# One PSUM tile takes its bank from another pool, and the sigmoid table is loaded in a later block

## The chip, the cores and the metric

The kernel runs on one core of one Trainium2 chip. The metric is the device time of one execution in microseconds (us). The engines are named as in the profile: PE (TensorE matmuls), PEld (its weight loads), DVE (VectorE), ACT (ScalarE), POOL (GpSimd) and SP (SyncE, which issues the DMAs here). Each engine works through its own instructions in order; it waits for the others by semaphores.

## What is computed

An attention (2 batches, 8 heads, 768 positions, 64 per head; each query sees a window of keys and 24 block summaries) is followed by two MLPs over 1536 tokens, all in float32:

```python
def _moe_ref(x, w_in, w_out):            # first MLP
    h = np.maximum(x @ w_in, 0.0)        # 1536x512 @ 512x2048
    return (h * h @ w_out)               # 1536x2048 @ 2048x512

def _moe2_ref(x, w_in, w_out):           # second MLP
    h = x @ w_in
    g = h * (1.0 / (1.0 + np.exp(-h)))
    return (g @ w_out)

def reference(...):
    attn_out = _attn_ref(q, k, v)        # scores, exp, normalise, times v
    x = attn_out.transpose(0, 2, 1, 3).reshape(B * S, H * D)
    return _moe2_ref(_moe_ref(x, ...), ...)
```

## The kernel before

Every float32 factor is split into a high and a low part, and each product is three matmuls (high by high, high by low, low by high).

The first MLP is done in three token blocks of 512 columns. `first_block` (block 1 of 3, to about 151 us) runs the attention for its own tokens and the 16 chunks of the MLP beside it; its order is written out by a planner (`first_order`). `layer1_block(1, ...)` (the second block, to about 257 us) runs beside the rest of the attention, and `layer1_block(2, ...)` (the third block, to about 350 us) runs beside the decoding of the second MLP's weights (`prefetch`). In each chunk m a product `h` (12 matmuls, PSUM pool `ps_h`) goes through ACT and DVE into `g`, and two chunks later `g` times `wo` is added into four accumulators (`ps_acc`). The last accumulations of the third block are kept back in the list `fill`.

The second MLP runs over 16 steps q: eight pairs of 128 hidden columns for each of two token groups of 768. Its first product uses seven half-size products of a Strassen-like scheme, which run in a chain through two or three PSUM tiles per step: `hx` (products 11, s2, s3 and 22), `hz` (s1 and s4) and `hy` (12). Each product is six matmuls of 128x384; `evacuate` copies the intermediate states of the chain to SBUF (ACT, tiles `e`), DVE adds them, and `silu` makes four quarters of `g` (sigmoid on ACT, a multiplication on DVE, high part on ACT, low part on DVE). The last quarter, `s21`, reads `hx` itself, so `hx` is in use until the DVE multiplication of `s21`. Between the products, `between` puts the accumulations of the step before, `rows(q-1, k)` for k = 0 to 5, or in step 0 the pieces kept in `fill`. `rows` multiplies the quarters of `g` by `wq`, the split of the second MLP's output weights (`load2`: a DMA, high part on ACT, low part on DVE). `ready` splits the weights of the next step into `r` (high part on ACT, low part on DVE).

PE's order in the third block and the second MLP is the order in which the code is written; the order of ACT and DVE there is a scheduler's.

PSUM has eight banks, in three pools (lines 238 to 240), and a tile here fills one:

```python
ps_h   = ... bufs=2     # h of the first MLP; hx, hz, hy of the second
ps_acc = ... bufs=4     # accumulators, k = 0, 1, 2, 5 in the second MLP
ps_att = ... bufs=2     # attention; accumulators k = 3, 4 in the second MLP
```

A new tile of a pool waits until the last reader of the bank's former tile is done.

ACT evaluates its functions from a loaded table. Line 902, `act.activation(out=share[:, 0:1], in_=share[:, 0:1], func=AF.Sigmoid)`, is written ahead of the third block and computes nothing that is used: `share` is a small constant tile whose readers are done by then. It is there so that a table with the sigmoid is loaded. It depends on little, and the order of the built kernel has it early in the first block.

Of the kernel before, what the change touches and what calls it, by code (L numbers as in the profile page):

```python
# [10 lines left out]
F32 = mybir.dt.float32  # L11
F32R = mybir.dt.float32r
AF = mybir.ActivationFunctionType
# [9 lines left out]
P = 128  # L23
# [27 lines left out]
HALF = 384  # L51
# [157 lines left out]
def kernel(  # L209
# [17 lines left out]
    vec, act, pool, pe, sp = nc.vector, nc.scalar, nc.gpsimd, nc.tensor, nc.sync  # L227
# [10 lines left out]
    ps_h = ctx.enter_context(tc.tile_pool(name="ps_h", bufs=2, space=PSUM))  # L238
    ps_acc = ctx.enter_context(tc.tile_pool(name="ps_acc", bufs=4, space=PSUM))
    ps_att = ctx.enter_context(tc.tile_pool(name="ps_att", bufs=2, space=PSUM))  # L240
# [9 lines left out]
    def tt(eng, o, a, b, op):  # L250
        return eng.tensor_tensor(out=o, in0=a, in1=b, op=op)  # L251

    def sub(eng, o, a, b):
        return tt(eng, o, a, b, ALU.subtract)
# [26 lines left out]
    def raw_wi(w, m, name):  # L281
        load_raw(w[m].rearrange("p k f -> p (k f)"), f"{name}{m}")
# [4 lines left out]
    def dec_scale(name):  # L287
        c = ws_p.tile([P, DM], I32, tag="c", name=f"c_{name}")

        copy(act, c.bitcast(F32), raws[name][:, :, 1].bitcast(F32), scale=2.0 ** -112)  # L290
        return c

    def dec_low(name):
        low = raws[name][:, :, 0]
        vec.tensor_scalar(out=low, in0=low, scalar1=29, scalar2=None, op0=ALU.logical_shift_right)

    def dec_sign(name):
        low, high = raws[name][:, :, 0], raws[name][:, :, 1]
        vec.scalar_tensor_tensor(out=low, in0=high, scalar=SIGN, in1=low,  # L299
                                 op0=ALU.bitwise_and, op1=ALU.bitwise_or)  # L300
# [45 lines left out]
    share = share_p.tile([P, PHASE - 8], F32, tag="share", name="share")  # L346
# [147 lines left out]
    def att_steps():  # L494
        for i in range(NFIRST - 1, NG + 2):
            if NFIRST <= i - 2 < NG:
                products(i - 2)
                x_high(i - 2)
                x_low(i - 2)
            if i + 1 < NG:  # L500
                kw_load(i + 1)
                q_load(i + 1)
                side_by_side(i + 1)
                k_sums(i + 1)
            if NFIRST <= i < NG:
                v_load(i)
            yield
            if NFIRST <= i - 1 < NG:
                transposes(i - 1)
                a_copy(i - 1)  # L510
            yield
            if NFIRST <= i < NG:
                scores(i)
                minima(i)
                exps(i)
                guard(i)
                inverse(i)
                norm(i, vec)
            yield

    att = att_steps()
# [62 lines left out]
    def first_block():  # L584
# [172 lines left out]
        finish1(0, accs)  # L757

    def layer1_block(bi, steps, prefetch, last=None):
        n = BLOCKS[bi]  # L760
        x = xt[bi]
# [33 lines left out]
    def keep_decoded(j):  # L795
        name = f"wp{j}"
        raw_wo(w_out2, j, "wp")
        c = dec_scale(name)
        dec_low(name)
        dec_sign(name)  # L800
        dec_join(name, c)
        sp.dma_start(out=scr2[j], in_=c.bitcast(F32))
# [68 lines left out]
    def decode_pair(m):  # L871
        p, half = m // 2, m % 2
        name = f"wj{m}"
        if not half:
            us[p] = wi_p.tile([P, 2, 2, 2 * P], F32, tag="wi", name=f"u{p}")
        raw_wi(w_in2, m, "wj")
        c = dec_scale(name)
        dec_low(name)
        dec_sign(name)
        u = us[p]  # L880
        vec.scalar_tensor_tensor(out=u[:, half].rearrange("p a c -> p (a c)").bitcast(I32), in0=c, scalar=3, in1=raws.pop(name)[:, :, 0],
                                 op0=ALU.logical_shift_left, op1=ALU.bitwise_or)
        if half:
            v = vs[p] = wi_p.tile([P, 3, 2 * P], F32, tag="wi", name=f"v{p}")
            tt(pool, v[:, 0], u[:, 1, 0], u[:, 1, 1], ALU.add)
            sub(pool, v[:, 1], v[:, 0], u[:, 0, 0])
            sub(pool, v[:, 2], u[:, 0, 1], v[:, 1])
            sub(pool, u[:, 1, 0], u[:, 0, 0], u[:, 1, 0])

    parts = build(lambda name: raw_p.tile([P, 2, HALF], F32, tag="raw", name=name))  # L890

    def prefetch(m):
        decode_pair(m)
        if m >= 3 and m - 3 < 5:
            parts[m - 3]()
        elif m == 8:
            parts[5]()
        if m >= 10 and FIRST2 + DEC1 <= FIRST2 + DEC1 + m - 10 and DEC1 + m - 10 < NF:
            keep_decoded(DEC1 + m - 10)

    fill = [None]
    act.activation(out=share[:, 0:1], in_=share[:, 0:1], func=AF.Sigmoid)
    with tc.manual_schedule(engines={pe.engine}):
        layer1_block(2, 0, prefetch, fill)
        fill = fill[1:]
        xt2_ctx.close()
# [21 lines left out]
        def product(o, q, x, first):  # L928
            r, f = ring.pop((q, x)), forms[TIMES[x]].bitcast(F32R)
            for kk in range(2):  # L930
                w = slice(kk * P, kk * P + P)
                mm(o, r[:, 0, w], f[:, 0, kk], start=first and kk == 0, stop=False, skip_group_check=not first)
                mm(o, r[:, 0, w], f[:, 1, kk], start=False, stop=False, skip_group_check=not first)
                mm(o, r[:, 1, w], f[:, 0, kk], start=False, stop=kk == 1, skip_group_check=not first)
            ready(q + 1, x)

        def evacuate(src, name):
            e = ev_p.tile([P, HALF], F32, tag="ev", name=name)
            copy(act, e, src)
            return e  # L940

        def silu(src, g, cols, name):
            s = s_p.tile([P, HALF], F32, tag="s", name=name)
            act.activation(out=s, in_=src, func=AF.Sigmoid)  # L944
            tt(vec, s, src, s, ALU.mult)
            on_act = copy(act, g[:, 0, cols], s)
            marks_done.append((on_act, sub(vec, g[:, 1, cols], s, g[:, 0, cols].bitcast(F32))))
# [3 lines left out]
        def load2(n):  # L951
            if n < 2 * NF:
                c = c_p.tile([P, DM], F32, tag="c", name=f"c2_{n}")
                sp.dma_start(out=c, in_=scr2[n % NF])
                w = wo2[n] = w_p.tile([P, 2, DM], F32R, tag="w", name=f"wq{n}")
                with behind(1):
                    split(w, c, vec)
# [18 lines left out]
        def between(q, ks):  # L976
            if q > 0:
                for k in ks:
                    rows(q - 1, k)
            elif fill:  # L980
                fill.pop(0)()
# [14 lines left out]
        def again(x):  # L996
            sp.dma_start(out=forms[x], in_=kept[list(TIMES.values()).index(x)])
# [8 lines left out]
        for q in range(2 * NPAIR):  # L1006
            for i in range(2):
                gs[q, i] = gq_p.tile([P, 2, 2 * HALF], F32R, tag="g", name=f"g{q}_{i}")

            def after(i):  # L1010
                if q == NPAIR - 1:
                    again(TIMES[CHAIN[i]])

            xx = ps_h.tile([P, HALF], F32, tag="h", name=f"hx{q}")
            product(xx, q, "11", True)
            r1 = evacuate(xx, f"e1_{q}")
            after(0)
            z = ps_h.tile([P, HALF], F32, tag="h", name=f"hz{q}")
            product(z, q, "s1", True)
            r5 = evacuate(z, f"e5_{q}")  # L1020
            after(1)
            between(q, [3])
            product(xx, q, "s2", False)
            r2 = evacuate(xx, f"e2_{q}")
            after(2)
            product(z, q, "s4", False)
            tt(vec, r2, z, r2, ALU.add)
            silu(r2, gs[q, 0], b, f"s12_{q}")
            after(3)
            load2(2 * q)  # L1030
            between(q, [4, 5])
            product(xx, q, "s3", False)
            tt(vec, r5, xx, r5, ALU.add)
            silu(r5, gs[q, 1], b, f"s22_{q}")
            after(4)
            z = ps_h.tile([P, HALF], F32, tag="h", name=f"hy{q}")
            product(z, q, "12", True)
            tt(vec, r1, z, r1, ALU.add)
            silu(r1, gs[q, 0], a, f"s11_{q}")
            after(5)  # L1040
            load2(2 * q + 1)
            between(q, [0])
            product(xx, q, "22", False)
            silu(xx, gs[q, 1], a, f"s21_{q}")
            after(6)
            for x in ahead.get(q, []):
                stage(*x)
            between(q, [1, 2])
            if q:
                for i in range(2):  # L1050
                    gs.pop((q - 1, i))
# [69 lines left out]
```

## Time and profile before

| | us |
|---|---|
| median of 3 runs | 604.89 (604.69 to 605.63) |
| the profiled execution | 602.92 |
| span of its instructions | 601.1 |
| PE busy | 587.2 (98%) |
| DVE busy | 432.4 (72%) |
| ACT busy | 378.1 (63%) |
| POOL busy | 88.9 (15%) |

Times of rows are counted from the start of the span. The profiled execution took 1.8 us more than its span, and its own time is 2.0 us below the median of the runs that are compared; a difference worked out from its rows is taken off the median. "[x <-Y]" at a row's end says that the engine sat idle x us before it and what ended that.

### The profile page before, as it was taken

How to read it: one execution, taken by the hardware profiler on the slowest of the kernel's cores; microseconds unless marked ns; L12 is line 12 of the kernel's file. 1: busy time of each engine (PE TensorE's matmuls, PEld its weight loads, DVE VectorE, ACT ScalarE, POOL GpSimd, SP SyncE). 2: the span in 40 equal slices, each digit the busy share in tenths (PEclk: the TensorE clock that was granted, in tenths of full speed). 3: DMA queues.
4: the chain of work that ended last, by engine and by line, in shares of the span. 5: the costliest groups of instructions: out<-in, count | busy, mean ns of one | idle time of the engine just before them, and what ended most of it. 6: DMA issues, size and time to landing. Idle time of an engine off the chain costs nothing.

```text
span 601.1 us, 9565 instructions
## 1 busy us (share of the span) xinstructions
PE 587.2 (98%) x3300; PEld 492.2 (82%) x3300; DVE 432.4 (72%) x1007; ACT 378.1 (63%) x882; POOL 88.9 (15%) x93
## 2 busy tenths in 40 slices
PE   8989999999999999999999989999999999999997
PEld 6478777777787787888888879888999888999995
DVE  5989999992786776369965766777776766666542
ACT  5999986886655545366544766566655655555532
POOL 0000000002634443156623200000000000000000
PEclk9999999999999999999999999999999999999999
DMA  9987898765499887644683112232229520011102
GB/s 308 297 235 279 286 311 276 251 192 198 141 360 333 271 280 262 242 133 152 244 284 98 35 36 87 75 128 69 82 91 358 200 70 24 29 38 36 35 19 105
DMA packets 42240, 104.42 MB, mean 174 GB/s; under 512 B 4560, under 2 KB 11856, under 8 KB 42192
## 3 DMA queue, kind: packets, MB, share of 16 engines
q1 hardware_dynamic: 42192, 103.81, 51.5%
q8 instruction: 26, 0.43, 0.3%
q14 instruction: 22, 0.18, 0.1%
HBM read 78.37 MB, written 25.43 MB: 173 GB/s over the span
## 4 chain that ended last, share of the span: by engine, by line
PE 78%; DVE 5%; DMA 3%; ACT 1%; issue 0%; DVEq 0%; ACTq 0%
PE acc L243 38%; PE h L243 16%; PE hx L243 11%; PE hz L243 6%; PE hy L243 3%; PE pss L243 2%; DMA t_kv<-in_vT_dram 2%; PE av L243 1%; PE psa L453 1%; DMA kw<-in_kW_dram 1%; DVE g L251 1%; DVE vsumT L678 1%; DMA scr_dram<-c_wo 1%; DVE raw_wo L299 0%; DVE c_wi L303 0%; DVE c_wo L303 0%
## 5 line engine op out<-in xcount | busy, mean ns | idle before, releaser
L243 PE MATMUL h<-xt,wi 128*128 128x512 f32 x576 | 143.1, 395 | 0.0
L243 PE MATMUL acc<-wq,g 128*128 128x512 f32 x576 | 142.4, 392 | 0.0
L243 PE MATMUL acc<-g,wo 128*128 128x512 f32 x576 | 141.4, 393 | 0.3 <-DVE g L251 0.3
L243 PEld LDWEIGHTS acc<-g,wo 128*128 128x128 f32 x576 | 107.1, 188 | 23.8 <-DVE g L251 0.9
L243 PEld LDWEIGHTS h<-xt,wi 128*128 128x128 f32 x576 | 106.2, 188 | 23.2 <-issue 0.6
L243 PEld LDWEIGHTS acc<-wq,g 128*128 128x128 f32 x576 | 107.2, 188 | 19.6
L251 DVE TENSOR_TENSOR g<-r,g 128x512 fp32r<-128x512 f32 x48 | 37.6, 783 | 32.3 <-POOL r L251 18.5
L251 DVE TENSOR_TENSOR r_s<-v,r_s 128x256 fp32r<-128x256 f32 x48 | 20.2, 424 | 50.3 <-ACT r_s L247 50.3
L247 ACT ACTIVATE g<-s 128x384 fp32r<-128x384 f32 x64 | 33.2, 520 | 22.6 <-DVE s L251 22.6
L251 DVE TENSOR_TENSOR g<-s,g 128x384 fp32r<-128x384 f32 x64 | 35.5, 556 | 15.5 <-ACT g L247 13.8
L416 ACT ACTIVATE T<-T,m 128x120 f32<-128x120 f32 x96 | 36.7, 384 | 12.4 <-DVE m L411 12.2
L247 ACT ACTIVATE e<-hx 128x384 f32<-128x384 f32 x32 | 15.7, 492 | 44.9 <-PE hx L243 44.9
L243 PE MATMUL hx<-x_t,r_s 128*128 128x384 f32 x192 | 38.9, 337 | 0.0
L243 PEld LDWEIGHTS hx<-x_t,r_s 128*128 128x128 f32 x192 | 34.5, 188 | 2.7
L944 ACT ACTIVATE s<-e 128x384 f32<-128x384 f32 x48 | 25.2, 525 | 15.5 <-DVE e L251 15.4
L251 DVE TENSOR_TENSOR s<-e,s 128x384 f32<-128x384 f32 x48 | 26.5, 553 | 6.3 <-ACT s L944 6.2
L537 ACT ACTIVATE r<-h 128x512 f32<-128x512 f32 x16 | 9.6, 598 | 32.2 <-PE h L243 32.2
L248 POOL COPY qd<-qr 128x256 f32<-128x256 f32 x8 | 6.6, 820 | 147.0 <-DMA qr<-in_qW_dram 138.2
L247 ACT ACTIVATE r<-u 128x256 fp32r<-128x256 f32 x48 | 19.6, 408 | 11.9 <-PE hx L243 11.7
L251 POOL TENSOR_TENSOR wo<-c_wo,wo 128x512 fp32r<-128x512 f32 x16 | 24.1, 1505 | 6.9 <-ACT wo L247 6.5
L251 POOL TENSOR_TENSOR r<-r 128x512 f32<-128x512 f32 x16 | 17.4, 1091 | 47.5 <-ACT g L542 47.5
L411 DVE CUSTOM_DVE_ANT_0 T<-pss,cst_sb 128x120 f32<-128x120 f32 x96 | 21.9, 275 | 1.4 <-PE pss L243 1.1
(119 smaller groups left out, 978.4 us busy)
## 6 DMA issues: line engine op xcount, KB each, us to landing
raw_wi<-in_w_in_dram SPq DMA_DIRECT2D x16, 512.0 KB, 5.1
raw_wo<-in_w_out_dram SPq DMA_DIRECT2D x16, 512.0 KB, 5.1
raw_wp<-in_w_out_dram SPq DMA_DIRECT2D x16, 512.0 KB, 5.5
split<-wo SPq DMA_DIRECT2D x16, 512.0 KB, 3.6
raw_wj<-in_w_in_dram SPq DMA_DIRECT2D x16, 512.0 KB, 4.8
wo<-split SPq DMA_DIRECT2D x16, 512.0 KB, 4.4
c<-scr_dram SPq DMA_DIRECT2D x32, 256.0 KB, 2.6
scr_dram<-c_wo SPq DMA_DIRECT2D x16, 256.0 KB, 3.2
```

The costliest lines, as they stand in the source:

```text
L243: pe.matmul(o, l, r, **kw)
L247: return act.activation(out=o, in_=i, func=AF.Copy, scale=scale)
L248: return eng.tensor_copy(out=o, in_=i)
L251: return eng.tensor_tensor(out=o, in0=a, in1=b, op=op)
L411: vec.tensor_tensor_reduce(out=d["T"][:, c], in0=d["ps"][:, c], in1=cst_sb[:, kind * NK:kind * NK + NK], scale=-0.125, scalar=3.0e38, op0= ...
L416: act.activation(out=d["T"][:, c], in_=d["T"][:, c], func=AF.Exp, bias=d["m"][:, c:c + 1], scale=-1.0, accum_out=d["z"][:, c:c + 1])
L453: pe.transpose(ps[0:NK, c], d["T"][:, c], id_sb)
L537: act.activation(out=r, in_=h, func=AF.Relu)
L678: vec.tensor_reduce(out=sums[:, hp, i * n:(i + 1) * n], in_=halves.pop(j).rearrange("p (n j) -> p n j", j=KBLK), op=ALU.add if w else ALU. ...
L944: act.activation(out=s, in_=src, func=AF.Sigmoid)
```

## The change

```diff
     def prefetch(m):
+        if m == 2:
+            act.activation(out=share[:, 0:1], in_=share[:, 0:1], func=AF.Sigmoid)
         decode_pair(m)
...
     fill = [None]
-    act.activation(out=share[:, 0:1], in_=share[:, 0:1], func=AF.Sigmoid)
     with tc.manual_schedule(engines={pe.engine}):
         layer1_block(2, 0, prefetch, fill)
...
-            xx = ps_h.tile([P, HALF], F32, tag="h", name=f"hx{q}")
+            xx = (ps_h if q else ps_att).tile([P, HALF], F32, tag="h" if q else "att", name=f"hx{q}")
             product(xx, q, "11", True)
```

In step 0 the tile `hx` now lies in a bank of `ps_att`, and the sigmoid on `share` is written into the third block's chunk 2. (Line 944 of before is line 945 of after.)

ACT in the first block, ahead of the first copies of the attention's output (`av`, in PSUM) into `xt`, the input of the first MLP. One piece of the difference:

```order
 L247 ACTIVATE vlead_112<-psv0_124 24x2048 x2
-L902 ACT_TABLE_LOAD
-L902 ACTIVATE share_92<-share_92 128x1
 L247 ACTIVATE xt0_88<-av0_508 128x4x64
 L247 ACTIVATE xt0_88<-av1_519 128x4x64
@@ -69,5 +67,4 @@
 L247 ACTIVATE c_wi3_733<-raw_wi3_621 128x512
 L247 ACTIVATE c_wo3_748<-raw_wo3_645 128x512
-L416 ACT_TABLE_LOAD
 L416 ACTIVATE T8_750,z8_752<-T8_750,m8_751 128x120 x4
 L247 ACTIVATE wi3_767<-c_wi3_733 128x512
```

Both table loads of this stretch are gone: the sigmoid's and that of the exponentials that follow (`T8`, the ninth tile of the attention).

ACT in the third block's chunks 1 and 2 in the kernel after (`c_wj2` is the first step of decoding a weight chunk; `r2_2` and `g2_2` are chunk 2's relu, square and high part):

```order
L247 ACTIVATE g2_1_3056<-r2_1_3057 128x512
L894 ACT_TABLE_LOAD
L894 ACTIVATE share_92<-share_92 128x1
L247 ACTIVATE c_wj2_3099<-raw_wj2_3097 128x512
L537 ACTIVATE r2_2_3090<-h2_2_3076 128x512
```

The table load and the sigmoid on `share` stand here now; in the second MLP's step 0 the load of line 944 is gone.

PE around the end of step 0 and the start of step 1, before (`hx0`, `hx1`, `hz1`: the tiles of steps 0 and 1; `acc2_0_3`, `acc2_0_4`: accumulators of k = 3 and 4, in `ps_att`):

```order
L243 MATMUL hx1_3914<-x_b11_3001,r1_11_3786 128x384 [waits DVE_49]
L243 MATMUL hx1_3914<-x_b11_3001,r1_11_3786 128x384 x5
L243 MATMUL hz1_3926<-x_t1_3002,r1_s1_3798 128x384 [waits DVE_49]
L243 MATMUL hz1_3926<-x_t1_3002,r1_s1_3798 128x384 x5
L243 MATMUL acc2_0_3_3938<-wq0_3837,g0_0_3777 128x512 [waits PE_49,Activation_49]
L243 MATMUL acc2_0_3_3938<-wq0_3837,g0_0_3777 128x512 x2
L243 MATMUL acc2_0_3_3938<-wq1_3879,g0_1_3778 128x512 [waits Activation_49]
L243 MATMUL acc2_0_3_3938<-wq1_3879,g0_1_3778 128x512 x2
```

And after, with the first matmul into `acc2_0_4`:

```order
L243 MATMUL hx1_3914<-x_b11_3001,r1_11_3786 128x384 x6
L243 MATMUL hz1_3926<-x_t1_3002,r1_s1_3798 128x384 [waits DVE_49]
L243 MATMUL hz1_3926<-x_t1_3002,r1_s1_3798 128x384 x5
L243 MATMUL acc2_0_3_3938<-wq0_3837,g0_0_3777 128x512 [waits PE_49,Activation_49]
L243 MATMUL acc2_0_3_3938<-wq0_3837,g0_0_3777 128x512 [waits DVE_49]
L243 MATMUL acc2_0_3_3938<-wq0_3837,g0_0_3777 128x512
L243 MATMUL acc2_0_3_3938<-wq1_3879,g0_1_3778 128x512 [waits Activation_49]
L243 MATMUL acc2_0_3_3938<-wq1_3879,g0_1_3778 128x512 [waits DVE_49]
L243 MATMUL acc2_0_3_3938<-wq1_3879,g0_1_3778 128x512
```

The order of PE's matmuls is the same; the waits moved. `hx1` waits for nothing, `hz1` still waits for DVE, and `acc2_0_3` and (further on) the first matmul of `acc2_0_4` have waits for DVE that they did not need before. On ACT, the copy `e5_1` of `hz1` now stands ahead of the high part of `s21` of step 0; on DVE, one split for the next step stands ahead of the low part of `s21`. POOL's and SP's orders are the same.

## Rows read from the trace of the kernel before

**Rows 1.** The page, part 2: TensorE's granted clock in 40 slices of the span

```profile
PEclk9999999999999999999999999999999999999999
```

**Rows 2.** Waits of PE: engine line <- releaser: us in total, times, longest

```profile
PE hz L243 <- DVE s L251: 2.5, 1, 2.5
PE av L243 <- DVE xt L251: 1.7, 1, 1.7
...
PE pss L243 <- ACT vsum L247: 1.1, 1, 1.1
...
PE av L243 <- ACT a L247: 0.8, 1, 0.8
```

**Rows 3.** Timeline of ACT, first block: start us, us, operation, count

```profile
31.66 1.28 ACT L902 ACT_TABLE_LOAD   x1
32.96 0.20 ACT L902 ACTIVATE share<-share 128x1 f32<-128x1 f32 x1
33.19 0.94 ACT L247 ACTIVATE xt<-av 128x256 fp32r<-128x256 f32 x3
...
48.33 1.28 ACT L416 ACT_TABLE_LOAD   x1
```

**Rows 4.** Timeline of DVE, first block

```profile
31.59 0.42 DVE L295 TENSOR_SCALAR raw_wi<-raw_wi 128x512 int32<-128x512 int32 x1
33.60 1.09 DVE L251 TENSOR_TENSOR xt<-av,xt 128x256 fp32r<-128x256 f32 x3 [1.59 <-ACT xt L247]
...
51.28 0.17 DVE L436 TENSOR_SCALAR z<-z 128x4 f32<-128x4 f32 x1 [0.49 <-ACT T L416]
```

**Rows 5.** Timeline of PE, first block

```profile
30.31 2.08 PE L243 MATMUL av<-a,vlead 120*64 120x64 f32 x64
34.08 2.38 PE L243 MATMUL av<-a,vlead 120*64 120x64 f32 x64 [1.69 <-DVE xt L251]
```

**Rows 6.** Timeline of PE, second MLP, steps 1 and 2

```profile
351.58 1.21 PE L243 MATMUL hx<-x_b,r 128*128 128x384 f32 x6
355.33 1.31 PE L243 MATMUL hz<-x_t,r_s 128*128 128x384 f32 x6 [2.54 <-DVE s L251]
356.48 1.55 PE L243 MATMUL acc<-wq,g 128*128 128x512 f32 x6
357.87 1.21 PE L243 MATMUL hx<-x_t,r_s 128*128 128x384 f32 x6
...
370.01 1.23 PE L243 MATMUL hx<-x_b,r 128*128 128x384 f32 x6
371.08 1.20 PE L243 MATMUL hz<-x_t,r_s 128*128 128x384 f32 x6
```

**Rows 7.** Timeline of ACT, second MLP, steps 0 and 1

```profile
344.92 1.28 ACT L944 ACT_TABLE_LOAD   x1
...
350.38 0.42 ACT L247 ACTIVATE r<-u 128x256 fp32r<-128x256 f32 x1 [0.44 <-PE hx L243]
...
354.14 0.48 ACT L944 ACTIVATE s<-hx 128x384 f32<-128x384 f32 x1
```

**Rows 8.** Timeline of DVE, the same stretch

```profile
348.04 0.55 DVE L251 TENSOR_TENSOR e<-hy,e 128x384 f32<-128x384 f32 x1
...
353.79 0.68 DVE L251 TENSOR_TENSOR wq<-c,wq 128x512 fp32r<-128x512 f32 x1
...
354.72 0.55 DVE L251 TENSOR_TENSOR s<-hx,s 128x384 f32<-128x384 f32 x1
```

**Rows 9.** Timeline of ACT, third block, chunks 2 and 3

```profile
265.46 0.60 ACT L537 ACTIVATE r<-h 128x512 f32<-128x512 f32 x1 [0.22 <-PE h L243]
...
270.90 0.60 ACT L537 ACTIVATE r<-h 128x512 f32<-128x512 f32 x1 [2.11 <-PE h L243]
```

**Rows 10.** The chain that ended last, in order of time: a load in the first block

```profile
84.47 5.26 DMA t_kv<-in_vT_dram
```

**Rows 11.** The page, part 6: DMA issues, KB each, median us to landing

```profile
vrows<-in_vP_dram SPq DMA_DIRECT2D x3, 512.0 KB, 9.5
```

## The prediction

> **What bounds the kernel now.** I read PE's list of waits first, then the timelines of PE, ACT and DVE at the two places that the change touches. PE is busy for 98% of the span and has the full clock in all slices [rows 1], so only its idle time is to be won. That list is short, and its two largest rows are the two places of this change [rows 2]: 2.5 us once for hz, and 1.7 us once for av. Next come 1.1 us before the scores that wait for ACT's vsum, and 0.8 us before a product that waits for ACT's copy a.
>
> The wait of hz stands at 355.33 [rows 6]: hz1 follows hx1 and ends its wait with a DVE instruction s, which is the multiplication of s21 on hx0 at 354.72 [rows 8]. So hz1 takes over the bank of hx0. That multiplication is late because ACT's sigmoid on hx0 runs only at 354.14 [rows 7], behind nine other instructions, the first of which ACT began at 350.38, released by PE. The wait of av stands at 34.08 [rows 5]: the second four products of the attention need a bank of the first four, which DVE frees at 33.60 [rows 4], after ACT's first copy at 33.19 [rows 3]. Right ahead of that copy, ACT spends 31.66 to 33.19 on the table load and on the sigmoid on share.
>
> **Part 1: the bank of hx0.** With hx0 in a bank of the attention's pool, hz1 gets the bank of hy0, whose last reader is DVE's addition at 348.04 [rows 8], over long before. Without the wait, hz1 follows hx1 as it does in step 2: 371.08 - 370.01 = 1.07 us from start to start [rows 6]. So it starts at 351.58 + 1.07 = 352.65 instead of 355.33, which is 2.68 us earlier.
>
> What is late next? The wait had also covered the inputs of the accumulation acc2_0_3 behind it; the order of instructions shows waits for DVE there now. Its six matmuls begin one hz later, at 352.65 + 1.15 = 353.80 (1.15 = 356.48 - 355.33), and take 357.87 - 356.48 = 1.39 us, 0.23 each [rows 6]. The fifth needs the low part of the second weight tile, which DVE finishes at 353.79 + 0.68 = 354.47 [rows 8]; it starts at 353.80 + 4 x 0.23 = 354.72. The margin is 0.25 us. acc2_0_4 needs the bank of hx0, free at 354.72 + 0.55 = 355.27. It comes after acc2_0_3 (1.39) and twelve more matmuls of 128x384 (2 x 1.07), at 353.80 + 1.39 + 2.14 = 357.33, 2.1 us later. The copy of hz1 on ACT, which in the old order stood behind the high part of s21, is now ahead of it, right behind the sigmoid: 354.14 + 0.48 = 354.62 and one copy more, before hz is written again at 353.80 + 1.39 + 1.07 = 356.26. Should the margin of 0.25 us be missed, the fifth matmul waits, at worst until that same 355.27, which costs 0.55 us. So this part is worth 2.68 us, between 2.1 and 2.8; the upper end adds 0.1 for hz itself, which took 1.31 behind the wait and 1.20 without one [rows 6].
>
> **Part 2: the loads gone from the first block.** ACT loses 33.19 - 31.66 = 1.53 us ahead of its first copy of av. The copy can then start at 31.66, and DVE's subtraction 1.53 us earlier, at 32.07, for DVE is free at 31.59 + 0.42 = 32.01 [rows 4]. PE's second group then starts at 34.08 - 1.53 = 32.55; the first group was over at 34.08 - 1.69 = 32.39 [rows 5], so 0.16 us of the wait is left. Everything behind it in the first block (the low parts, the products h, the weight loads that SP issues when a raw buffer comes free) hangs on instructions of this stretch, not on a fixed time, so I let the whole shift through: 1.53 us.
>
> The second load, at 48.33, was needed because the exponentials found the sigmoid's table. It takes 1.28 us of ACT [rows 3]. PE does not wait there. DVE waited once, 0.49 us at 51.28, for these exponentials [rows 4], so it can gain that 0.49. DVE's work leads over two such loads (one is in [rows 10]) to the vsum for which PE waits 1.1 us. I take 0.49; the ends are 0 (PE or a load sets the pace) and 1.28 (all of the load, which the 0.8 + 1.1 us of PE's waits in [rows 2] could give back). The nearest row is DVE's wait, so its value.
>
> A rule bears on this price. The Trainium skill, "ScalarE: Activation LUTs", section "What ACT_TABLE_LOAD costs", gives a switch of tables 1283 ns for the load and about 1380 ns for a drain beside it, some 2.66 us. The row shows the 1283 ns, and the next ACT instruction follows 1.30 us after the load's start [rows 3], so the trace shows no drain of that length. By the page the wait of av would vanish altogether, at 1.69 instead of 1.53, and my sum would be larger by 0.16.
>
> **Part 3: the load put into the third block.** It stands between g of chunk 1 and the decoding of chunk 2: 33.19 - 31.66 = 1.53 us by the old place [rows 3]. The relu of chunk 2 then starts at about 265.46 + 1.5 = 267.0 and is over by 267.6. ACT's next wait is 2.11 us for PE, up to 270.90 [rows 9], and takes up the whole delay. PE needs that relu only when its bank is written again, which is after the product that ends at 270.90. Price: nothing, as long as this cover is there; without it, 1.53 us on ACT, and PE would still not wait.
>
> **Part 4: the load gone from step 0** (344.92, 1.28 us [rows 7]). ACT's stretch that makes s21 late starts at 350.38, when PE releases it [rows 7], not when the sigmoids are through. So this removal alone gives PE nothing.
>
> **Sum.** 2.68 + 1.53 + 0.49 + 0 + 0 = 4.70 us. On the profiled execution that is 602.92 - 4.70 = 598.2; on the median, which lies 2.0 above it, 604.89 - 4.70 = 600.2 us.
>
> **Rivals.**
> *The front shift is lost on the way.* The first block might be paced by its loads: the chain holds a load of 5.26 us for which DVE waits [rows 10]. Against it: that load is issued when DVE frees its buffer, so it moves along. If it holds, only part 1 is left: 604.89 - 2.68 = 602.2.
> *The wait moves instead of going.* acc2_0_3 now has its own waits, with 0.25 us to spare, while ACT and DVE are busy without a gap from 350.38 on. If the ACT or DVE stretch slips by 1.5 us in the new order, part 1 brings some 1.2 instead of 2.68: 604.89 - 1.2 - 1.53 - 0.49 = 601.7.
> *The change does not reach the end.* Both parts are given back, the first block's at a load and step 0's at the next tile of the bank: 604.9.
> *Slower, by loads that collide.* ACT and DVE free the weight buffers earlier, so SP issues 512 KB loads ahead of the small ones of t_kv, and DVE waits for them twice on the chain. A load that shared the engines with others took 9.5 us in the median (vrows [rows 11]) against 5.26 [rows 10]. Twice 4.2 us more is 8.5: 604.89 - 4.70 + 8.5 = 608.7. It decides from 3.0 us a load on (2 x 3.0 = 4.70 + 1.2). Against it: SP issues in the same order as before, and what frees the buffers moves by the same 1.5 us as what asks for the loads.
> *The page's drain.* A load takes the engine's pipe with it, and the first block wins the whole 1.69: 600.0.
>
> **How the numbers follow.** Forecast 600.2: chance 0.62. Front lost, 602.2: 0.14. Wait moved, 601.7: 0.10. Drain, 600.0: 0.03. No change: 0.06. Slower: 0.05. The low end takes all upper bounds, 2.8 + 1.69 + 1.28 = 5.8: 599.1, less the 0.2 by which the fastest of the three runs lies below their median: 598.9. The high end is the first rival, 602.2, with the 0.7 by which the slowest run lies above it: 602.9. Outside are no change and slower, 0.11, and what the measurement adds. A measurement of this kernel can tell about 0.2% from no change, 1.2 us. All cases but the last two are faster by more than that: 0.89; within, 0.06; slower, 0.05.
>
> **What would show it.** Right: PE's row for hz waiting for s gone from the list of waits, hz1 about 1.07 us behind hx1, and no new wait of acc above 0.3; the second group of av starting near 32.5, with a wait of about 0.2; two table loads instead of four; the scores that wait for vsum some 2.0 us earlier in the span than before; the relu of chunk 3 in the third block still waiting for PE. Wrong: the first product of the second block starting at its old distance from the span's start (front lost), acc waiting behind hz1 (wait moved), DVE waits for t_kv of more than 3 us (loads collide).

## The result, and the profile after

The changed kernel took 597.67 us (597.31 to 598.38, four executions) against 604.79 (603.73 to 605.63) for the kernel before, a ratio of 0.9889 [0.9862, 0.9916]. That is 2.5 us below the forecast and 1.2 us below the low end of its range. Measured twice more (below), it took 600.01 us with a ratio of 0.9924 [0.9902, 0.9946], and 597.80 with 0.9901 [0.9878, 0.9924]. The 16 executions together have a median of 597.97 us; the 77 executions of the kernel before that ran beside the experiments below have 604.19. By these medians the change is worth about 6.2 us (5.7 by the means of the same executions), where 4.70 was forecast.

| us | before | after |
|---|---|---|
| median, all executions | 604.19 (77) | 597.97 (16) |
| profiled execution | 602.92 | 597.49 |
| its span | 601.1 | 595.7 |
| executions with a mean granted clock of 0.998 or less | 57 of 77 | 2 of 16 |
| median of the others | 603.18 (20) | 597.71 (14) |

The granted clock is the share of its full clock that TensorE had; its mean over each execution is on record. The two profiled executions differ by 602.92 - 597.49 = 5.43 us. PE's waits after (engine, line, releaser: us in total, times, longest), which answer to [rows 2]:

```profile
PE idle_out L243 <- DVE idle_in L592: 1.5, 1, 1.5
PE pss L243 <- ACT vsum L247: 1.1, 1, 1.1
PE psa L453 <- DVE T L447: 1.0, 1, 1.0
PE psa L453 <- ACT T L445: 0.2, 1, 0.2
PE av L243 <- DVE xt L251: 0.2, 1, 0.2
```

The 2.5 us of hz are gone, of the 1.7 of av 0.2 is left, and the 0.8 of av for ACT's copy is gone too. There is no wait of acc, so nothing took hz's place. The timeline of PE after at the end of step 0 (start us, us, operation, count), against [rows 6]:

```profile
348.90 1.21 PE L243 MATMUL hx<-x_b,r 128*128 128x384 f32 x6
349.95 1.20 PE L243 MATMUL hz<-x_t,r_s 128*128 128x384 f32 x6
350.99 1.60 PE L243 MATMUL acc<-wq,g 128*128 128x512 f32 x6
352.42 1.21 PE L243 MATMUL hx<-x_t,r_s 128*128 128x384 f32 x6
```

hz follows hx by 1.05 us. From hx1 to the next hx it was 357.87 - 351.58 = 6.29 us before [rows 6] and is 352.42 - 348.90 = 3.52 now: part 1 brought 2.77. The other 2.68 were there already at hx1, 351.58 - 348.90, and nearly all of them came from the first block. PE there after, with the row of the scores that wait for vsum:

```profile
30.47 2.08 PE L243 MATMUL av<-a,vlead 120*64 120x64 f32 x64
32.72 2.37 PE L243 MATMUL av<-a,vlead 120*64 120x64 f32 x64 [0.17 <-DVE xt L251]
...
111.79 1.22 PE L243 MATMUL pss<-kw,qr 64*64 64x120 f32 x16 [1.07 <-ACT vsum L247]
```

and the same scores before:

```profile
114.39 1.22 PE L243 MATMUL pss<-kw,qr 64*64 64x120 f32 x16 [1.10 <-ACT vsum L247]
```

This execution began 0.16 us later (30.47 against 30.31 [rows 5]). Counted from its first group of av, the second group is 34.08 - 32.72 + 0.16 = 1.52 us earlier than before, the scores 114.39 - 111.79 + 0.16 = 2.76, and hx1 2.68 + 0.16 = 2.84. So 1.2 to 1.3 us were won behind the second group. The timeline of DVE after shows where the first of it came from:

```profile
32.24 1.09 DVE L251 TENSOR_TENSOR xt<-av,xt 128x256 fp32r<-128x256 f32 x3
...
41.62 0.43 DVE L295 TENSOR_SCALAR raw_wi<-raw_wi 128x512 int32<-128x512 int32 x1 [0.43 <-DMA raw_wi<-in_w_in_dram]
...
44.50 0.42 DVE L295 TENSOR_SCALAR raw_wo<-raw_wo 128x512 int32<-128x512 int32 x1
...
49.12 0.16 DVE L436 TENSOR_SCALAR z<-z 128x4 f32<-128x4 f32 x1
...
98.98 1.23 DVE L678 TENSOR_REDUCE vsumT<-t_kv 128x12 f32<-128x384 f32 x2 [0.53 <-DMA t_kv<-in_vT_dram]
```

Against [rows 4] the first of these is 1.36 us earlier, and z 51.28 - 49.12 = 2.16, without its wait: 0.80 of it is there at z. Before, DVE had two more waits for transfers here:

```profile
46.08 0.43 DVE L295 TENSOR_SCALAR raw_wo<-raw_wo 128x512 int32<-128x512 int32 x1 [0.65 <-DMA raw_wo<-in_w_out_dram]
...
101.79 1.02 DVE L678 TENSOR_REDUCE vsumT<-t_kv 128x12 f32<-128x384 f32 x2 [1.24 <-DMA t_kv<-in_vT_dram]
```

The 0.65 is gone (0.43 at 41.62 stands for it), and the 1.24 became 0.53. ACT after, first the two places of the first block, then the third block:

```profile
31.83 0.94 ACT L247 ACTIVATE xt<-av 128x256 fp32r<-128x256 f32 x3
...
47.09 0.40 ACT L416 ACTIVATE T<-T,m 128x120 f32<-128x120 f32 x1
...
262.01 1.28 ACT L894 ACT_TABLE_LOAD   x1
263.31 0.20 ACT L894 ACTIVATE share<-share 128x1 f32<-128x1 f32 x1
263.42 0.69 ACT L247 ACTIVATE c_wj<-raw_wj 128x512 f32<-128x512 f32 x1
...
268.23 0.60 ACT L537 ACTIVATE r<-h 128x512 f32<-128x512 f32 x1 [0.91 <-PE h L243]
```

Neither load of [rows 3] is there. The one of the third block costs ACT 1.41 us, and its wait for PE behind it fell from 2.11 [rows 9] to 0.91 us: ACT still waits for PE, and PE has no wait there.

### The profile page after: what moved, and what is told of

Same layout as the page of the kernel before. It is cut to its first block, busy times and chain, and to the rows that moved or that the text cites. A ratio compares the mean times of both kernels' runs of the same rounds, so it can differ in the third digit from the quotient of the medians.

```text
span 595.7 us, 9564 instructions
## 1 busy us (share of the span) xinstructions
PE 587.4 (99%) x3300; PEld 492.5 (83%) x3300; DVE 431.9 (73%) x1007; ACT 375.6 (63%) x880; POOL 91.8 (15%) x93
## 4 chain that ended last, share of the span: by engine, by line
PE 79%; DVE 5%; DMA 3%; ACT 1%; issue 0%; SPq 0%; DVEq 0%; ACTq 0%
PE acc L243 39%; PE h L243 17%; PE hx L243 11%; PE hz L243 6%; PE hy L243 3%; PE pss L243 2%; DMA t_kv<-in_vT_dram 2%; PE av L243 1%; PE psa L453 1%; DMA kw<-in_kW_dram 1%; DVE g L251 1%; DVE raw_wo L299 1%; DVE c_wi L303 1%; DVE c_wo L303 1%; DVE vsumT L678 0%; DVE ksum L678 0%
## 5 line engine op out<-in xcount | busy, mean ns | idle before, releaser
L251 DVE TENSOR_TENSOR g<-r,g 128x512 fp32r<-128x512 f32 x48 | 35.8, 747 | 30.9 <-POOL r L251 17.0
```

## Experiments

The first three, and the first of the two repeats of the changed kernel, ran beside the same 23 executions of the kernel before (median 604.05 us); the last two ran beside 13 (604.02), the others beside 29 (604.37).

**The bank alone.**

```diff
-            xx = ps_h.tile([P, HALF], F32, tag="h", name=f"hx{q}")
+            xx = (ps_h if q else ps_att).tile([P, HALF], F32, tag="h" if q else "att", name=f"hx{q}")
```

> The bank of hx0 alone; the sigmoid stays ahead of the third block, and its load in the first block. Theory of parts that add: PE's wait of 2.5 us at hz goes and nothing takes its place, so the time is 2.7 us below the kernel before (1.07 us from hx1 to hz1, as in step 2), and the first block is as before: the wait of av stays at 1.7, the four table loads stay. Rival (wait moves): acc2_0_3 waits behind hz1 because ACT still has the load of 1.28 us in step 0; then only about 1.2 us are won. Rival (the part is worth more in the timed runs than in one profile): 4 us or more.

It took 600.03 us (six executions), 0.9936 [0.9923, 0.9949]: 3.9 us less, not 2.7, and nearly the 4 of the second rival. In its trace hz follows hx by 1.04 us, and the four loads are there. So the timed executions gained over a microsecond more than PE's row said. The traced spans differ by 3.5 (601.1 and 597.6): 2.79 lie between hx1 and the next hx, and 0.74 ahead of hx1, which the bank does not touch. Those 0.74 are a difference between two executions. DVE's row for z, which before waited 0.49 us for the second load [rows 4], is here

```profile
50.87 0.17 DVE L436 TENSOR_SCALAR z<-z 128x4 f32<-128x4 f32 x1 [1.21 <-ACT T L416]
```

**The loads alone.**

```diff
     def prefetch(m):
+        if m == 2:
+            act.activation(out=share[:, 0:1], in_=share[:, 0:1], func=AF.Sigmoid)
...
-    act.activation(out=share[:, 0:1], in_=share[:, 0:1], func=AF.Sigmoid)
```

> The sigmoid table alone in the third block; hx0 stays in its old bank. Theory of parts that add: 1.5 us from the copies of av, which start 1.5 us earlier, and 0.5 (my prediction) to 1.3 us (all of the second load, as the changed kernel's trace suggests) from the load that the exponentials no longer need: 2.0 to 2.8 us below the kernel before, all of it there by the start of the second block; hz1 still waits 2.5 us, since ACT's stretch before it starts when PE releases it. Rival (front lost at the loads): under 0.7 us. Rival (the timed runs gain more than the profile): 4 us or more.

The span of the profiled execution fell from 601.1 to 598.5, by 2.6; but the twelve executions run from 600.16 to 605.47 us, median 602.59, 0.9973 [0.9955, 0.9991], so by 1.6 us of 604. That is less than the 2.0 to 2.8 expected, but the interval (0.5 to 2.7 us) does not exclude them. The wait of hz stays at 2.54.

**No sigmoid ahead of the third block at all**, so that its table is loaded in step 0, as before.

```diff
-    act.activation(out=share[:, 0:1], in_=share[:, 0:1], func=AF.Sigmoid)
```

> The sigmoid on share is left out altogether; nothing that is used changes. The first block is that of the changed kernel, and the sigmoid's load stands in step 0 of the second MLP, as before. If that load is off the path, as I put it, the time is the same as with the table moved alone, within 0.5 us. If the load in step 0 costs PE something, this kernel is up to 1.3 us slower than that one, with a longer wait at hz.

601.70 us, 0.9968 [0.9947, 0.9989], again with a wide spread (599.49 to 605.77). The load of 1.28 us stands at 341.67 in step 0, and PE's wait of hz is 2.54 as in the kernel that has no load there; in the trace of the bank alone, which has that load too, hz does not wait at all. So the traces show no cost of it for PE. The medians of this kernel and of the loads alone are 0.9 us apart, more than the 0.5 expected; with such spreads that decides nothing.

**The changed kernel twice more.**

> The changed kernel again, beside its two parts. Theory of parts that add: its gain is the sum of the gains of the two parts alone, 2.7 plus 2.0 to 2.8 us, within 0.6 us. Rival (the parts need each other): more than the sum by over 1 us, as the first measurement's 7.1 us of medians against 5.4 us between the two profiled executions would have it.

> The changed kernel once more. Its first measurement gave 597.7 us from four runs, the second 600.0 from six, with the same span of 595.3 to 595.7 in the profiled execution. Theory A (the prediction's sum is right, and the four runs were all short ones of a kernel that spreads by 4 us): the median is again within 1 us of 600, and the ratio to before is 0.991 to 0.994. Theory B (the kernel is worth 7 us and the second measurement was disturbed): near 597.7, ratio 0.989. The trace should again show the scores that wait for vsum within 0.3 us of 111.8 and no wait of hz.

600.01 and 597.80 us, with scores behind vsum at 111.17 and 111.45. The second fits the first measurement (theory B), the first the forecast; its executions run from 597.11 to 601.54. Its gain of 4.0 by medians is less than that of the two parts alone together (3.9 and 1.6), so the parts did not add there; the traced spans nearly do (5.8 against 3.5 and 2.6). What separates them is not in the profiled executions, whose spans are 595.3 and 595.4.

**Both loads at the front.**

```diff
     act.activation(out=share[:, 0:1], in_=share[:, 0:1], func=AF.Sigmoid)
+    act.activation(out=share[:, 0:1], in_=share[:, 0:1], func=AF.Exp)
```

> The kernel before with an exponential on the same constant tile right behind the sigmoid of the first block. Both table loads then stand ahead of ACT's first copy of av, and the one at 48.33 [rows 3] is gone. It prices the second load against the first: the front gets about 1.5 us later (a load of 1.28 and 0.2 for the exponential), and what the second load cost is given back. Theory A (the second load is worth DVE's 0.49, as the prediction took it): the scores that wait for vsum, at 114.39 us in the trace of before, start 1.0 us later, near 115.4, and the time is 1.0 us above before. Theory B (it is worth about 1.2, for it also decides how long DVE waits for a load of weights and for t_kv): they start near 114.7, and the time is 0.3 us above before.

604.93 us, 1.0018 [1.0003, 1.0034]. PE in its trace:

```profile
31.18 2.08 PE L243 MATMUL av<-a,vlead 120*64 120x64 f32 x64
36.36 2.99 PE L243 MATMUL av<-a,vlead 120*64 120x64 f32 x64 [3.10 <-DVE xt L251]
...
115.69 1.22 PE L243 MATMUL pss<-kw,qr 64*64 64x120 f32 x16 [1.10 <-ACT vsum L247]
```

Counted from the first group of av, the second is (36.36 - 31.18) - (34.08 - 30.31) = 1.41 us later than before, and the scores (115.69 - 31.18) - (114.39 - 30.31) = 0.43. The second load's going gave back 1.0 us up to the scores, and 1.2 up to hx1 (352.63 here), as theory B had it. As they stand, though, the start of the scores and the time, 1.1 us above before by the ratio, are those of theory A. The first group of av began 0.87 us later in this execution, and the clock has a share in the time, below: all twelve executions have a mean of 0.998 or less, eight of them of 0.994 or less, against 6 of the 77 of the kernel before.

**The sigmoid behind the copies of av**, with the bank changed.

```diff
+            if (what, arg) == ("xh", NLEAD - 1):
+                act.activation(out=share[:, 0:1], in_=share[:, 0:1], func=AF.Sigmoid)
...
-    act.activation(out=share[:, 0:1], in_=share[:, 0:1], func=AF.Sigmoid)
```

> The bank of hx0 changed as in the changed kernel, and the sigmoid of the first block moved behind ACT's copies of the eighth attention tile instead of into the third block. The front ahead of the first copy of av is then free of the load, but both loads stay in the first block, since the exponentials load their table again, and the load of step 0 is as before. Against the kernel with the bank alone this is worth the front's 1.5 us. Against the changed kernel it lacks what the second load is worth. Theory A (0.49): the scores that wait for vsum, at 111.79 us in the trace of the changed kernel, start near 112.3. Theory B (1.2): they start near 113.0. If the load in the new place delays the high parts of x or the weights that follow it, they start later still, up to 114.

Neither theory held: the scores start later even than the 114 allowed for a load that delays what follows it. PE's timeline, then the new waits in DVE's:

```profile
30.52 2.08 PE L243 MATMUL av<-a,vlead 120*64 120x64 f32 x64
32.75 2.37 PE L243 MATMUL av<-a,vlead 120*64 120x64 f32 x64 [0.15 <-DVE xt L251]
...
114.58 1.22 PE L243 MATMUL pss<-kw,qr 64*64 64x120 f32 x16 [1.10 <-ACT vsum L247]
```

```profile
37.75 0.69 DVE L303 SCALAR_TENSOR_TENSOR c_wi<-c_wi,raw_wi 128x512 int32<-128x512 int32 x1 [1.27 <-ACT c_wi L247]
51.33 0.17 DVE L436 TENSOR_SCALAR z<-z 128x4 f32<-128x4 f32 x1 [1.31 <-ACT T L416]
```

The time is 600.40 us, 0.9949 [0.9929, 0.9968], no better than with the bank alone. The wait of av became one of 1.27 us at c_wi, and from the first group of av to the scores it takes 84.06 us, against 84.08 before. The stretches of the kernel before say why (us of the stretch, then PE, PEld, DVE, ACT and POOL busy; clock, DMA share, GB/s):

```profile
25.00:35.00 10.00, 7.28 (x112) 4.51 (x112) 8.23 (x30) 9.94 (x24) 0.00 (x0) 1.00 1.06 332
35.00:45.00 10.00, 9.77 (x99) 8.05 (x95) 9.93 (x22) 9.86 (x20) 0.00 (x0) 1.00 0.70 221
45.00:60.00 15.00, 15.00 (x68) 12.37 (x67) 13.73 (x37) 14.76 (x33) 0.00 (x0) 1.00 0.79 279
```

ACT is busy for 34.56 of these 35 us. The load cost as much at its new place (35.67) as at the old one (31.66); at av it was only seen first.

**The kernel before against itself.**

> The kernel before against itself, for the size of what such a comparison can tell. Theory A (all kernels spread from execution to execution for reasons that are not in the program): ratio 1.000 within 0.002, with runs between 603 and 607. Theory B (only kernels without the table loads in the first block spread by more than 3 us): runs within 603 to 605.5.

1.0006 [0.9989, 1.0022], with executions from 602.35 to 606.33: theory A, a little wider at the low end. This profiled execution, at a mean clock of 0.996, is one of the long ones: its span is 604.5, 3.4 us more than the 601.1 of the trace that the prediction read. Up to hx1 (353.36 against 351.58) it lost 1.78: PE waits 1.4 us for psa there, and DVE 2.25 and 1.53 us for t_kv instead of 0.58 and 1.24. The other part stands in its stretches around hz:

```profile
354.00:356.00 2.00, 0.57 (x4) 0.25 (x2) 2.00 (x5) 2.00 (x6) 0.00 (x0) 1.00 0.01 2
356.00:358.00 2.00, 0.89 (x4) 0.89 (x5) 1.41 (x4) 0.94 (x3) 0.00 (x0) 0.89 0.71 184
358.00:360.00 2.00, 2.00 (x7) 1.81 (x6) 0.29 (x2) 0.80 (x2) 0.00 (x0) 0.50 0.20 76
360.00:362.00 2.00, 2.00 (x9) 1.68 (x9) 0.34 (x1) 0.00 (x0) 0.00 (x0) 0.76 0.00 0
```

and in PE's timeline:

```profile
357.11 1.94 PE L243 MATMUL hz<-x_t,r_s 128*128 128x384 f32 x6 [2.54 <-DVE s L251]
358.84 2.53 PE L243 MATMUL acc<-wq,g 128*128 128x512 f32 x6
361.21 1.23 PE L243 MATMUL hx<-x_t,r_s 128*128 128x384 f32 x6
```

Behind the wait of 2.54 us the granted clock falls to 0.50, the lower of its two levels, and is back at 362. From hz to the next hx it takes 361.21 - 357.11 = 4.10 us, against 357.87 - 355.33 = 2.54 in [rows 6]: 1.56 more.

**The wait of hz kept, the loads gone, once more; and both loads in front with the bank changed.** The two ask whether the clock falls behind waits or at fixed places. The second kernel is the one with both loads at the front and the bank's line.

> The change of the table loads alone, once more, for the clock behind the wait of hz, which stays in this kernel. Theory A (most executions lose 1.6 us at a lower clock right behind that wait): if the mean clock of the profiled execution is 0.997 or less, the granted clock is near 0.5 in the 2 to 5 us behind hz, and 1.00 through the first block, where av waits less than 0.3 us. If the mean is 0.999, the clock is 1.00 there. Theory B (the lower means come from elsewhere): a lower mean with 1.00 behind hz.

> Both loads ahead of ACT's first copy of av, as in the run that put an exponential behind the sigmoid there, and the bank of hx0 changed. PE's wait of av is then about 3.1 us long and its wait of hz is gone. Theory A (a long wait of PE, wherever it stands, is followed by some us at a lower granted clock): the clock falls behind av, near 37 to 41 us, and not behind hz. The mean clock is 0.996 to 0.997 in most executions and never 0.993, and the time is 4.2 us below the same kernel without the bank's change (2.7 for the wait, 1.6 for the clock behind it), near 600.7. Theory B (the falls belong to stretches of the program, not to the waits): the clock falls near 360 us as well, with means down to 0.993, and the time is 2.7 us below, near 602.2.

The first, a single execution, took 605.6 us at a mean of 0.994. Its stretches, in the first block and around hz:

```profile
30.00:32.00 2.00, 0.38 (x4) 0.32 (x3) 1.95 (x9) 2.00 (x2) 0.00 (x0) 1.00 1.08 300
32.00:34.00 2.00, 2.00 (x47) 1.82 (x48) 1.97 (x5) 1.98 (x3) 0.00 (x0) 0.82 0.97 242
34.00:36.00 2.00, 2.00 (x44) 2.00 (x42) 1.87 (x6) 1.78 (x6) 0.00 (x0) 0.50 0.77 176
...
356.00:358.00 2.00, 1.58 (x7) 1.52 (x8) 0.92 (x2) 0.68 (x2) 0.00 (x0) 0.89 0.41 146
358.00:360.00 2.00, 2.00 (x6) 1.60 (x5) 0.42 (x1) 0.64 (x2) 0.00 (x0) 0.50 0.00 0
360.00:362.00 2.00, 2.00 (x10) 1.91 (x10) 0.00 (x0) 0.22 (x1) 0.00 (x0) 0.76 0.00 0
```

There is the same fall behind hz, and one in the first block that theory A had not expected, behind a wait of 1.62 us for psa. The second took 601.67 us, 0.9950 [0.9931, 0.9969], with means from 0.991 to 1.000. In its profiled execution (0.992) PE waits 1.83 and 1.63 us for psa, and the clock is at 0.54 from 34 to 36 us and at 0.50 from 36 to 44. So it fell ahead of av's wait, which is 1.98 us here and not 3.1. In both traces DVE had waited for raw_wi shortly before (1.46 us in the first, 2.79 in the second). Around hz, which no longer waits, it stays at the full level:

```profile
356.00:358.00 2.00, 2.00 (x12) 1.82 (x11) 1.81 (x4) 2.00 (x6) 0.00 (x0) 1.00 0.00 0
358.00:360.00 2.00, 2.00 (x12) 1.71 (x11) 2.00 (x5) 2.00 (x6) 0.00 (x0) 1.00 0.30 63
```

That agrees with theory A, but one trace can't show it, for four of the six traces with the wait of hz have no fall there. The mean clocks of all executions say more. Without both loads at the front, 74 of 102 executions of kernels in which hz waits have a mean of 0.998 or less (before, the loads alone, no sigmoid), and 5 of 34 of those in which it does not (changed, the bank alone, the sigmoid behind av). So the fall goes with the wait. That the mean would be 0.996 to 0.997 in most executions and never 0.993, and the 600.7 us, were wrong: three of the ten have 0.994 or less, the trace shows that the first block can lose more than expected, and the 601.67 us lie nearer to the 602.2 of theory B.

## Why the prediction was wrong in size

The direction, the places and the mechanism were right; two steps were too small: the price of the second load, and the step from the profiled execution to the median. Of the 2.5 us by which the forecast missed, each accounts for 0.7 to 0.8. The other 1.0 or so is luck: the first comparison, of four executions each, shows 7.1 us where all executions together show 6.2.

1. **Part 1 in the profiled execution: right.** 2.68 forecast, 2.77 measured from hx to hx. hz took 1.20, as the 0.1 in the upper end had allowed. The margin of 0.25 us for acc held, and the rival of the moved wait fell.

2. **The step from the profiled execution to the median: too small.** The prediction knew that the profiled execution lay 2.0 below the median, and took the same difference off both. It read "full clock in all slices" [rows 1] for the kernel, where it held for that execution (a digit of 9 means 0.9 or more over 15 us). Of 77 executions of the kernel before, 57 have a mean of 0.998 or less, among them the traced one that lost 1.56 us behind hz. The wait so has a second price, which goes with it: the changed kernel has 2 such executions of 16, and the counts above show that this follows the wait of hz, not the loads. Where the clock stays up on both sides, the medians are 603.18 and 597.71, 5.47 apart, as the two profiled executions are (5.43). Within the kernel before, the 57 have a median of 604.56, 1.4 above the other 20. The remaining 0.75 of the 6.2 (0.84 by means) is the share of such executions. An estimate from these numbers: 1.56 x (57/77 - 2/16) = 0.96. That all of the 57 fell behind hz is argued, not shown: one trace of this kernel and one of the loads alone show where. A mean of 0.998, which two of the 57 have, is no sure sign either: the traced execution of the kernel without the sigmoid has it, and its clock is down only at the end of the span, behind PE's last work. The bank alone gained 3.9 instead of 2.7, which fits in part.

3. **The front load: 1.53 forecast, 1.52 at av.** The reason was too narrow, though. The prediction priced the wait that it could see at av; moving the load behind av took that wait away and brought nothing. ACT, busy for 34.56 of 35 us, is the bound there.

4. **The second load: the mis-sized term.** 0.49 was taken, for DVE's wait in [rows 4], with 1.28 as the upper end. By the scores it is 2.76 - 1.52 = 1.24, and by hx1 2.84 - 1.52 = 1.32. With both loads at the front it came to 1.0 and 1.2. As waits for transfers differ between executions, more traces are needed for the size. From the first group of av to the scores it takes 83.5 to 84.1 us in three traces with both loads in this stretch (before, the bank alone, the sigmoid behind av; 85.9 in the long execution of before), and 80.5 to 81.7 in five without (three of the changed kernel, the loads alone, no sigmoid). The means, 83.9 and 81.2, are 2.7 apart, which leaves 1.2 for the second load. In the kernel with the bank alone the same wait of DVE is 1.21 us long, and DVE does not wait for raw_wo there; before, the two waits are 0.65 + 0.49 = 1.14. The row chosen showed only what another wait had left over. Both loads together cost ACT 1.53 + 1.28 = 2.81 us, and 2.76 came back. The forecast argued that "PE does not wait there", but DVE and the transfers behind it pass the delay on to vsum.

5. **Parts 3 and 4: right at nothing.** The third block's cover held, and hz waited 2.54 us with the load in step 0 and without it.

6. **The other rivals.** Lost front, no change and slower fell: DVE's longest wait for t_kv is 0.56 to 0.81 us in the three traces of the changed kernel, not 3. (That rival's 4.2 us compared unlike loads: vrows has 512 KB, t_kv 192.) The drain also fell. The Trainium skill ("ScalarE: Activation LUTs", "What ACT_TABLE_LOAD costs") gives a switch of tables 2.66 us; by an estimate from this figure, two loads would have returned up to 5.3. They returned 2.76, and the trace after has the next instruction 263.31 - 262.01 = 1.30 us behind a load's start.

With 1.24 for the second load the sum is 5.45, against the 5.43 between the two profiled executions, and with the clock's 0.96 it is 6.4. The range failed because it took its ends from one execution's rows and added 0.2 for the spread.

Left open is why two measurements of the same kernel lie 2.2 us apart. They ran on two chips, but the kernel before differs by only 0.3 us between these (604.05 and 604.37). Some executions of 599.9 and 601.5 us have a mean clock of 1.000, so the clock is not all of it; the long execution of the kernel before points to waits for t_kv and psa, but no long execution of the changed kernel was traced.

## What to carry to other kernels

A stall's price is not only its row in one trace: compare the profiled execution with the spread of the others, clock included, before its difference is taken off a median. Where an engine is busy through a stretch and the others end up waiting for it, an instruction that is removed from it can be worth its whole length (here 2.76 of 2.81 us), wherever the first wait happens to show, and moving it within the stretch can bring nothing. When a term is bounded by a wait, look whether another wait just ahead of it has hidden a part.

## What the runs showed of the hardware

After waits of PE of 2.54 us the granted clock fell to its lower level for some 3.4 us (an estimate from the 0.89, 0.50 and 0.76 of three stretches of 2 us) in two of the six traces that have the wait of hz, and not in the other four: the same program can run either way. Falls also followed waits of 3.10 us (both loads at the front: 0.50 from 38 to 40 us), of 1.62 us for psa (the loads alone, second trace), and of 1.83 and 1.63 us for psa (both loads at the front with the bank changed); in the trace of before the wait of 1.69 us [rows 5] was followed by none. The table loads took 1.28 us of ACT, and the next instruction began 1.30 us after a load's start (before at 31.66, after at 262.01).
